# Loading and transposing the first sequence's z in three parts, and regrouping the first score tiles

## The chip, the core and the metric

The kernel runs on one core of a Trainium2 chip. The metric is the time of one execution on the device in microseconds: a median of 980.89 over three runs (980.73 to 981.65). The engines named below: TensorE (PE in the profile, its weight loads PEld), VectorE (DVE), ScalarE (ACT), GpSimd (POOL) and SyncE (SP). SP and POOL issue the DMAs, which all use the core's 16 DMA engines.

## What is computed

Eight sequences of 3072 rows each; z has 64 columns, u and v have 256. A squared-ReLU attention of z with itself, gated by u, is followed by a two-branch feed-forward layer.

```python
def _attn_ref(u, v, z):
    scores = (1.0 / S) * np.matmul(z, z.transpose(0, 2, 1))
    attn = np.maximum(scores, 0.0) ** 2
    return u * np.matmul(attn, v)

def _moe_ref(x, w1, w2, w_out):
    return np.maximum(x @ w1, x @ w2) @ w_out
```

The inputs are 32-bit floats in DRAM; the kernel computes in bf16 with 32-bit sums.

## The kernel before

**Tiles and steps.** A sequence is cut into 24 blocks of 128 rows. Four blocks of queries make a step, so there are six steps for a sequence and 48 in all. A step needs its scores against all 24 key blocks. Scores are made two key blocks at a time: a *pair* `k0` (key blocks k0 and k0+1) against the step's 512 queries, in one PSUM tile. The pair is passed through ReLU (ScalarE, or VectorE for a few pairs at the start, lines 215 to 218), then squared on VectorE (line 221) into `a_sb`. Then come four matmuls that add the pair's contribution to the two sums `xacc` (one for each half of v's 256 columns): I call them *adds*; they show as `xacc<-a_sb,v_sb`. Because the score matrix is symmetric, later steps reuse earlier pairs, turned by DMA transposes (`aT`).

**zT.** Scores need z transposed. `zT` has 25 slots of 128 x 128; slot s holds block s-1 in its lower 64 rows and block s in its upper 64. Scoring a pair with an even `k0` takes its weights from slot k0+1 and the first step's queries from slots 0 to 4. For later sequences zT is made by two DMA transposes (`make_zT`). For sequence 0 it is made by TensorE, with an identity matrix, in `zT_pe` (matmuls at line 134, the copy out of PSUM at line 135).

**The start, sequence 0.** SP loads the first nine blocks of z as 32-bit floats (line 336). POOL builds the identity, loads the other 15 blocks with a cast (line 342), then the six parts of v (four blocks each) and u for the first step. VectorE and ScalarE cast the nine blocks (lines 343 and 344). TensorE runs idle matmuls on a blank tile (`idle`), transposes slots 0 to 8, runs four more idle matmuls, scores pairs 0 and 2, transposes slots 9 to 24, and scores pairs 4 and 6; the order is written out by hand in lines 624 to 660.

**The order of the rest.** `work` is the list of work items in TensorE's order; an item of the first step is one key block, two adds. Score tiles are grouped into *windows* (lines 502 to 508): the first three windows have two pairs each, all later ones three. A planner gives each window a place in `work` ahead of which it is issued (`laid`). Windows 0 and 1 are issued by hand; window 2 (pairs 8 and 10) is `third()`, issued ahead of item 2. Windows 3 (pairs 12, 14, 16), 4 (18, 20, 22) and 5 stand ahead of items 6, 12 and 18. PSUM has three buffers (`mm_psum`) for score tiles and transposes; a buffer comes free when its ReLU or its copy has read it. TensorE takes its matmuls in program order.

**Transfers.** Loads and transposes of the later steps are planned by time (`plan`). A planned load on POOL first waits, in `gate`, for the tile that was made last (`fresh`), then is issued. SP's queue holds, in order, the first load of z, the transpose of u for the first step (`uT`), four `aT` transposes, and so on.

Of the kernel before, what the change touches and what calls it, by code (L numbers as in the profile page):

```python
# [11 lines left out]
def kernel(  # L12
# [17 lines left out]
    nc = tc.nc  # L30
    fp32 = mybir.dt.float32
    bf16 = mybir.dt.bfloat16
# [4 lines left out]
    dqk = z.shape[-1]  # L37
    Dff = moe_w1.shape[-1]

    P = 128  # L40
    NSB = S // P
    G = 4
    WIN = 3
# [12 lines left out]
    zepool = ctx.enter_context(tc.tile_pool(name="zepool", bufs=1))  # L56
# [11 lines left out]
    mm_psum = ctx.enter_context(tc.tile_pool(name="mm_psum", bufs=3, space=bass.MemoryType.PSUM))  # L68
    acc_psum = ctx.enter_context(tc.tile_pool(name="acc_psum", bufs=1, space=bass.MemoryType.PSUM))

    pin = tc.keep_in_program_order

    def matmul(*args, **kw):
        pin(nc.tensor.matmul(*args, **kw))  # L74

    def sp_dma(**kw):
        pin(nc.sync.dma_start(**kw))
# [7 lines left out]
    def load(**kw):  # L85
        pin(nc.gpsimd.dma_start(**kw))
# [16 lines left out]
    def new_v():  # L103
        return vpool.tile([P, NSB, D], bf16, name="v_sb")

    def load_v(b, v_sb, t0, n):
        load(
            out=v_sb[:, ds(t0, n), :],
            in_=v[b].rearrange("(p t) d -> p t d", p=P)[:, ds(t0, n), :],
        )  # L110

    def load_u(b, c):
        u_sb = ulpool.tile([P, G, D], bf16, name="u_sb")
        load(
            out=u_sb,
            in_=u[b].rearrange("(p t) d -> p t d", p=P)[:, ds(c * G, G), :],
        )
        return u_sb
# [10 lines left out]
    def zT_pe(zT, z_sb, s0, n, tpz=None):  # L129
        flat = z_sb.rearrange("p t d -> p (t d)")  # L130
        if tpz is None:
            tpz = mm_psum.tile([P, 8, P], bf16, name="tpz", tag="mm")
        for j in range(n):
            pin(nc.tensor.transpose(tpz[:, j, :], flat[:, ds((s0 + j) * dqk, P)], ident))  # L134
        return lambda copy: pin(copy(zT[:, ds(s0, n), :], tpz[:, :n, :]))
# [50 lines left out]
    def direct(b, i, j):  # L186
        return b == 0 and i < j <= NDIR


    def score(q, out_ps, j, k, s, q0, n):  # L190
        half = ds(j * dqk, dqk)
        matmul(
            out_ps,
            q.zT[half, k + 1 - j, :],
            q.zT[half, ds(G * s + 1 - j + q0, n), :],
            start=True,
            stop=True,
        )

    def turn(out_ap, in_ap):  # L200
        sp_dma(out=out_ap, in_=in_ap, transpose=True)


    def scores_pair(b, s, k0):
        q = seqs[b]
        s_ps = mm_psum.tile([P, 2, GW], fp32, name="s_ps", tag="mm")
        for j in range(2):
            score(q, s_ps[:, j, :], j, k0 + j, s, 0, G)
        yield
        a_sb = apool.tile([P, 2, GW], bf16, name="a_sb")  # L210
        r_sb = apool.tile([P, 2, GW], bf16, name="r_sb", bufs=3)

        head = b == 0 and s == 0 and k0 < 12
        keep = pin if head else lambda ins: None
        if head and k0 in (2, 10):
            keep(nc.vector.tensor_single_scalar(out=r_sb, in_=s_ps, scalar=0.0, op=ALU.max))
        else:
            keep(nc.scalar.activation(r_sb, s_ps, AF.Relu))  # L218
        if head:
            yield  # L220
        keep(nc.vector.tensor_mul(a_sb, r_sb, r_sb))  # L221
        gj = k0 // G
        if gj > s and not direct(b, s, gj):
            if (s, gj) not in q.T:
                q.T[s, gj] = tpool.tile([P, G, G, P], bf16, name="aT")
            turn(
                q.T[s, gj][:, ds(k0 - G * gj, 2), :, :].rearrange("p k q x -> p (k q) x"),
                a_sb.rearrange("p j q -> p (j q)"),
            )
        yield a_sb  # L230
# [96 lines left out]

    q = seqs[0]  # L330
    ZF = 9
    blank = consts.tile([P, GW], bf16)
    pin(nc.vector.memset(blank, 0.0))
    zf = opool.tile([P, G, D], fp32, name="o_sb").rearrange("p t (n d) -> p (t n) d", d=dqk)
    z_in = z[0].rearrange("(p t) d -> p t d", p=P)
    sp_dma(out=zf[:, :ZF, :], in_=z_in[:, :ZF, :])
    ident = consts.tile([P, P], bf16)
    make_identity(nc, ident)
    z_sb_0 = zepool.tile([P, NSB + 2, dqk], bf16, name="z_sb")
    pin(nc.gpsimd.memset(z_sb_0[:, 0:1, :], 0.0))  # L340
    pin(nc.gpsimd.memset(z_sb_0[:, NSB + 1 : NSB + 2, :], 0.0))
    load(out=z_sb_0[:, 1 + ZF : 1 + NSB, :], in_=z_in[:, ZF:, :])
    pin(nc.vector.tensor_copy(z_sb_0[:, 1:6, :], zf[:, :5, :]))  # L343
    pin(nc.scalar.copy(z_sb_0[:, 6 : 1 + ZF, :], zf[:, 5:ZF, :]))
    q.v = new_v()
    for t0 in range(0, NSB, G):
        load_v(0, q.v, t0, G)
    q.u_sb[0] = load_u(0, 0)
    q.zT = zpool.tile([P, NSB + 1, P], bf16, name="zT")


    fresh = [None]
# [149 lines left out]
    windows, room = [], 0  # L502
    for i, (n, k0) in enumerate(tiles):
        if not room or (k0 is None and room < 2):
            windows.append([])
            room = 2 if i < 6 else WIN
        windows[-1].append((n, k0))
        room = 0 if (n + 1) % NG == 0 and k0 == -1 else room - 1

    begins, t = [], 0  # L510
# [9 lines left out]
    def free(at):  # L520
        return all(end <= at - 860 or at + 1700 <= beg for beg, end in shared)
# [5 lines left out]
    def apart(at):  # L527
        n = max(n for n, beg in enumerate(starts) if beg <= at)
        return n >= LAG or (at - starts[n]) % (6 * 432) == 0

    spots = [
        i
        for i, at in enumerate(begins)
        if free(at) and apart(at) and work[i][1] is False and work[i][0]
    ]
    GAP_FIRST, GAP = 2100, 2500
    n_first = sum(n < NG for n, _ in tiles) // WIN
    laid = {}
    limit = t
    for w in reversed(range(len(windows))):  # L540
        limit = min([limit] + [due[r] for r in windows[w] if r in due])
        found = [i for i in spots if begins[i] <= limit]
        i = found[-1] if found else 0
# [58 lines left out]
    def scores_window(w):  # L602
        gens = []
        for n, k0 in windows[w]:
            st = steps[n]
            if k0 is None:
                gens.insert(0, (st, k0, scores_diag(st.b, st.s)))
            elif k0 >= 0:
                gens.append((st, k0, scores_pair(st.b, st.s, k0)))
        for st, k0, gen in gens:  # L610
            next(gen)
        for st, k0, gen in gens:
            st.scored[k0] = a = next(gen)
            fresh[0] = a[:, 0, 0:1] if k0 is not None else a[:, 0, 0, 0:1]
# [4 lines left out]
    def idle(n):  # L619
        for _ in range(n):  # L620
            matmul(steps[0].xacc[0], blank[:, :P], blank, start=True, stop=True)


    laid = {i: [w for w in ws if w > 2] for i, ws in laid.items()}
    idle(6)
    parts = [zT_pe(q.zT, z_sb_0, 0, 5), zT_pe(q.zT, z_sb_0, 5, ZF - 5)]
    for part, copy in zip(parts, (nc.vector.tensor_copy, nc.scalar.copy)):
        part(copy)
    idle(4)
    heads = {k0: scores_pair(0, 0, k0) for w in range(3) for _, k0 in windows[w]}  # L630

    def ahead(*k0s):
        for k0 in k0s:
            next(heads[k0])

    def squared(*k0s):
        for k0 in k0s:
            steps[0].scored[k0] = a = next(heads[k0])
            fresh[0] = a[:, 0, 0:1]

    ahead(0, 2)
    ahead(0, 2)
    tpz = mm_psum.tile([P, 2, 8, P], bf16, name="tpz", tag="mm")
    parts = [zT_pe(q.zT, z_sb_0, ZF + 8 * i, 8, tpz[:, i]) for i in range(2)]
    squared(0)
    for part, copy in zip(parts, (nc.scalar.copy, nc.vector.tensor_copy)):
        part(copy)
    ahead(4)
    idle(1)
    ahead(6)  # L650
    idle(2)
    ahead(4, 6)
    squared(2, 4)

    def third():
        ahead(8, 10)
        ahead(8, 10)
        squared(6, 8, 10)

    laid.setdefault(spots[0] + 2, []).insert(0, -1)  # L660
    for i, (_, _, fn, _) in enumerate(work):
        for w in laid.get(i, []):
            scores_window(w) if w >= 0 else third()
        while transfers and transfers[0][0] <= begins[i]:
            _, _, is_load, begin_transfer = transfers.pop(0)
            if is_load:
                gate(fresh[0])
            begin_transfer()
        fn()
# [30 lines left out]
```

## Time and profile before

| | us |
|---|---|
| median of 3 runs (lowest, highest) | 980.89 (980.73, 981.65) |
| the profiled execution | 981.47 |
| its span on the core | 979.70 |

| where in the span | us |
|---|---|
| first idle matmul | 1.19 |
| nine blocks of z landed (288 KB, issued 0.74) | 3.67 |
| first transpose on TensorE | 4.17 |
| first scores (pairs 0 and 2) | 6.53 |
| second set of transposes, 16 | 7.06 |
| first adds (pair 0) | 9.47 |
| window 2 (pairs 8 and 10) | 10.43 |
| window 3 (pairs 12, 14, 16) | 12.80 |
| first load of u landed (issued 5.26) | 15.5 |
| first DMA transpose (uT) issued, landed | 15.52, 21.8 |
| uT first read (xT on VectorE) | 22.71 |

The page is one profiled execution: part 1 gives the busy time of each engine, part 4 the chain of work that ended last, part 6 the DMA issues with their median time from issue to landing. The timeline lists instructions in order of time, merged where they follow each other: start, duration, engine, line, operation and tiles. The DMA view of a stretch lists the queues that moved packets in it (q0 is POOL's, q1 is SP's), each with packets, megabytes and the share of 16 engines, and the DMAs whose issue falls in it.

### The profile page before, as it was taken

The page shows a single profiled execution, that of the slowest core. Times are in us where ns is not written, and L with a number is a line of the kernel's source. Part 1 is how long each engine was busy: PE and PEld are TensorE (multiplying, and loading weights), DVE is VectorE, ACT ScalarE, POOL GpSimd, SP SyncE. Part 2 cuts the span into 40 slices and gives each one's busy share as a digit, 9 for nine tenths or more (in the row PEclk, how much of TensorE's full clock was granted, in tenths as well). Part 3 has the DMA queues.
Part 4 walks back from the last instruction along what each step waited for, and adds up shares of the span by engine and source line. Part 5 has one row for each costly group of instructions (what it writes and reads, how often), then busy time and mean ns, then how long its engine had stood idle before and what let it go on. Part 6 is the DMA issues. An engine that isn't in the chain of part 4 may idle for free.

```text
span 979.7 us, 14514 instructions
## 1 busy us (share of the span) xinstructions
PE 968.9 (99%) x5661; PEld 510.6 (52%) x5742; DVE 432.0 (44%) x681; ACT 442.4 (45%) x500; POOL 77.5 (8%) x228
## 2 busy tenths in 40 slices
PE   9999999999999999999999999999999999999998
PEld 3355545555455554555545564455545555445556
DVE  6654444443544435433445334444345443554322
ACT  6853454334643355433554335533355433654322
POOL 2011100110001100010000100011000110000000
PEclk9999999999999999999999999999999999999999
DMA  9988899986989979898788968789777896896521
GB/s 150 186 142 150 145 180 153 165 147 114 182 161 149 150 118 180 152 168 130 150 157 144 175 122 164 142 153 181 135 147 149 135 188 126 148 164 115 109 66 65
DMA packets 378517, 143.46 MB, mean 146 GB/s; under 512 B 356944, under 2 KB 358608, under 8 KB 378448
## 3 DMA queue, kind: packets, MB, share of 16 engines
q1 hardware_dynamic: 361888, 112.78, 61.3%
q0 software_dynamic: 16560, 29.74, 21.5%
q8 instruction: 45, 0.74, 0.3%
q14 instruction: 24, 0.20, 0.1%
HBM read 59.77 MB, written 25.17 MB: 87 GB/s over the span
## 4 chain that ended last, share of the span: by engine, by line
PE 99%; issue 1%; DMA 0%; DVE 0%
PE xacc L74 52%; PE o_ps L74 21%; PE d_ps L74 17%; PE s_ps L74 8%; DMA o_sb<-in_z_dram 0%; PE tpz L134 0%; PE w2o_ps L74 0%; DVE o_sb L317 0%; DVE z_sb L343 0%
## 5 line engine op out<-in xcount | busy, mean ns | idle before, releaser
L74 PEld LDWEIGHTS <-v_sb 128*128 128x128 bf16 x2304 | 216.0, 98 | 277.4 <-issue 40.5
L218 ACT ACTIVATE r_sb<-s_ps 128x1024 bf16<-128x1024 f32 x258 | 248.5, 1023 | 111.4 <-PE s_ps L74 111.4
L221 DVE TENSOR_TENSOR a_sb<-r_sb 128x1024 bf16<-128x1024 bf16 x260 | 179.3, 691 | 212.1 <-ACT r_sb L218 207.9
L74 PE MATMUL xacc<-a_sb,v_sb 128*128 128x512 bf16 x997 | 231.0, 379 | 2.3 <-issue 0.2
L74 PE MATMUL xacc<-aT,v_sb 128*128 128x512 bf16 x912 | 216.5, 379 | 0.0
L74 PE MATMUL o_ps<-w_out_sb,g_sb 128*128 128x256 bf16 x1536 | 199.1, 273 | 0.0
L74 PE MATMUL d_ps<-xT,w_sb 128*128 128x512 bf16 x751 | 172.7, 379 | 0.9
L74 PEld LDWEIGHTS <-g_sb 128*128 128x128 bf16 x1536 | 149.9, 98 | 27.6
L292 ACT ACTIVATE g_sb<-d_ps 128x1024 bf16<-128x1024 f32 x96 | 98.3, 1024 | 138.8 <-PE d_ps L74 138.8
L292 DVE TENSOR_SCALAR g_sb<-d_ps 128x1024 bf16<-128x1024 f32 x96 | 117.4, 1223 | 84.7 <-PE d_ps L74 81.3
L323 ACT COPY o_sb<-o_ps 128x512 f32<-128x512 f32 x94 | 55.1, 586 | 178.2 <-PE o_ps L74 178.2
L268 DVE SCALAR_TENSOR_TENSOR xT<-xacc,uT 128x512 bf16<-128x512 f32 x96 | 62.0, 683 | 137.4 <-PE xacc L74 137.4
L74 PEld LDWEIGHTS <-w_sb 128*128 128x128 bf16 x768 | 75.1, 98 | 88.7
L74 PE MATMUL s_ps<-zT 64*128 64x512 bf16 (+3 forms) x696 | 89.2, 359 | 0.1
L246 ACT ACTIVATE r_sb<-s_ps 128x896 bf16<-128x896 f32 x44 | 40.3, 917 | 97.9 <-PE s_ps L74 97.9
L74 PE MATMUL xacc<-aD,v_sb 128*128 128x512 bf16 x331 | 79.9, 379 | 2.6 <-issue 2.2
L74 PE MATMUL o_ps<-W2o_sb,xT 128*128 128x256 bf16 x384 | 73.3, 273 | 0.0
L248 DVE TENSOR_SCALAR r_sb<-s_ps 128x384 bf16<-128x384 f32 x44 | 24.5, 558 | 95.3 <-PE s_ps L74 95.3
L74 PEld LDWEIGHTS <-zT 64*128 64x128 bf16 x696 | 27.2, 94 | 62.2 <-issue 50.4
L83 POOL COPY gate_sb<-g_sb 128x1 bf16<-128x1 bf16 x44 | 8.3, 188 | 420.0 <-DVE g_sb L292 253.2
L74 PEld LDWEIGHTS <-xT 128*128 128x128 bf16 x384 | 37.6, 98 | 4.4
L83 POOL COPY gate_sb<-a_sb 128x1 bf16<-128x1 bf16 x48 | 9.7, 203 | 273.9 <-DVE a_sb L221 273.9
(37 smaller groups left out, 144.2 us busy)
## 6 DMA issues: line engine op xcount, KB each, us to landing
out_dram<-o_sb SPq DMA_DIRECT2D x47, 512.0 KB, 3.7
v_sb<-in_v_dram POOLq DMA_DIRECT2D x48, 256.0 KB, 5.7
u_sb<-in_u_dram POOLq DMA_DIRECT2D x48, 256.0 KB, 5.3
aT<-a_sb SPq DMA_TRANSPOSE x228, 3.7
z_sb<-in_z_dram POOLq DMA_DIRECT2D x7, 384.0 KB, 7.5
aD<-aD SPq DMA_TRANSPOSE x132, 2.4
w_sb<-in_moe_w_dram POOLq DMA_DIRECT2D x2, 512.0 KB, 6.5
uT<-u_sb SPq DMA_TRANSPOSE x48, 4.8
```

What stands on the lines that cost most here:

```text
L74: pin(nc.tensor.matmul(*args, **kw))
L83: pin(nc.gpsimd.tensor_copy(gate_sb, tile_ap))
L218: keep(nc.scalar.activation(r_sb, s_ps, AF.Relu))
L221: keep(nc.vector.tensor_mul(a_sb, r_sb, r_sb))
L246: nc.scalar.activation(r_sb, s_ps[:, 0:7, :], AF.Relu)
L248: nc.vector.tensor_single_scalar(out=r2_sb, in_=s2_ps[:, 2:5, :], scalar=0.0, op=ALU.max)
L268: nc.vector.scalar_tensor_tensor(out=xT[:, dc, :].rearrange("p (t q) -> p t q", q=P), in0=xacc[dc].rearrange("p (t q) -> p t q", q=P), sca ...
L292: nc.any.tensor_single_scalar(out=g_sb[:, nb : nb + 2, :], in_=d_ps, scalar=0.0, op=ALU.max)
L323: nc.any.tensor_copy(o_sb[:, ds(2 * th, 2), :], o_ps[:, :, :D])
```

## The change

Sequence 0's z comes in three parts now. SP loads five blocks as 32-bit floats. POOL loads the next eight as its first instruction, ahead of building the identity, and the last eleven behind the first part of v. The load of u moves ahead of v's last two parts. The two edge slots of z are cleared by VectorE instead of POOL.

TensorE transposes slots 0 to 4 ahead of the scores of pairs 0 and 2, and slots 5 to 12 behind them. Slots 13 to 24 are filled by two DMA transposes on SP, odd slots first; they stand in SP's queue ahead of uT. The first three windows are pairs 0 and 2, pair 4, and pairs 6, 8 and 10. The third is still issued ahead of item 2; windows 3 and 4 are placed by hand ahead of items 8 and 14; the later windows stay where they were. Idle matmuls go from 13 to 7, and pair 10's ReLU goes from VectorE to ScalarE.

```diff
-        if head and k0 in (2, 10):
+        if head and k0 == 2:
             keep(nc.vector.tensor_single_scalar(out=r_sb, in_=s_ps, scalar=0.0, op=ALU.max))
...
-    ZF = 9
+    ZF, ZP = 5, 13
...
+    def load_z_0(t0, n):
+        load(out=z_sb_0[:, ds(1 + t0, n), :], in_=z_in[:, ds(t0, n), :])
+
     sp_dma(out=zf[:, :ZF, :], in_=z_in[:, :ZF, :])
+    load_z_0(ZF, ZP - ZF)
     ident = consts.tile([P, P], bf16)
     make_identity(nc, ident)
...
-    load(out=z_sb_0[:, 1 + ZF : 1 + NSB, :], in_=z_in[:, ZF:, :])
-    pin(nc.vector.tensor_copy(z_sb_0[:, 1:6, :], zf[:, :5, :]))
-    pin(nc.scalar.copy(z_sb_0[:, 6 : 1 + ZF, :], zf[:, 5:ZF, :]))
+    pin(nc.vector.memset(blank, 0.0))
+    pin(nc.vector.memset(z_sb_0[:, 0:1, :], 0.0))
+    pin(nc.vector.memset(z_sb_0[:, NSB + 1 : NSB + 2, :], 0.0))
+    pin(nc.vector.tensor_copy(z_sb_0[:, 1:4, :], zf[:, :3, :]))
+    pin(nc.scalar.copy(z_sb_0[:, 4 : 1 + ZF, :], zf[:, 3:ZF, :]))
     q.v = new_v()
-    for t0 in range(0, NSB, G):
+    load_v(0, q.v, 0, G)
+    load_z_0(ZP, NSB - ZP)
+    for t0 in range(G, 4 * G, G):
         load_v(0, q.v, t0, G)
     q.u_sb[0] = load_u(0, 0)
+    for t0 in range(4 * G, NSB, G):
+        load_v(0, q.v, t0, G)
     q.zT = zpool.tile([P, NSB + 1, P], bf16, name="zT")
+    for s0 in (ZP, ZP + 1):
+        n = (NSB + 2 - s0) // 2
+        sp_dma(
+            out=q.zT[:, s0 : NSB + 1 : 2, :],
+            in_=z_sb_0.rearrange("p t d -> p (t d)")[:, ds(s0 * dqk, n * P)],
+            transpose=True,
+        )
...
-            room = 2 if i < 6 else WIN
+            room = {0: 2, 2: 1}.get(i, WIN)
...
-    laid = {i: [w for w in ws if w > 2] for i, ws in laid.items()}
-    idle(6)
-    parts = [zT_pe(q.zT, z_sb_0, 0, 5), zT_pe(q.zT, z_sb_0, 5, ZF - 5)]
-    for part, copy in zip(parts, (nc.vector.tensor_copy, nc.scalar.copy)):
-        part(copy)
-    idle(4)
+    laid = {i: [w for w in ws if w > 4] for i, ws in laid.items()}
+    for k, w in ((2, -1), (8, 3), (14, 4)):
+        laid.setdefault(spots[0] + k, []).insert(0, w)
...
+    idle(4)
+    zT_pe(q.zT, z_sb_0, 0, ZF)(nc.vector.tensor_copy)
+    idle(1)
     ahead(0, 2)
     ahead(0, 2)
-    tpz = mm_psum.tile([P, 2, 8, P], bf16, name="tpz", tag="mm")
-    parts = [zT_pe(q.zT, z_sb_0, ZF + 8 * i, 8, tpz[:, i]) for i in range(2)]
+    part = zT_pe(q.zT, z_sb_0, ZF, ZP - ZF)
+    idle(2)
     squared(0)
-    for part, copy in zip(parts, (nc.scalar.copy, nc.vector.tensor_copy)):
-        part(copy)
+    part(nc.scalar.copy)
     ahead(4)
-    idle(1)
-    ahead(6)
-    idle(2)
-    ahead(4, 6)
-    squared(2, 4)
+    ahead(4)
+    squared(2)
 
     def third():
-        ahead(8, 10)
-        ahead(8, 10)
-        squared(6, 8, 10)
-
-    laid.setdefault(spots[0] + 2, []).insert(0, -1)
+        ahead(6, 8, 10)
+        ahead(6, 8, 10)
+        squared(4, 6, 8, 10)
```

More of the change, by code (lines that the diff above doesn't have):

```diff
@@ L330 @@
     q = seqs[0]
-    ZF = 9
+    ZF, ZP = 5, 13
     blank = consts.tile([P, GW], bf16)
-    pin(nc.vector.memset(blank, 0.0))
     zf = opool.tile([P, G, D], fp32, name="o_sb").rearrange("p t (n d) -> p (t n) d", d=dqk)
+    z_sb_0 = zepool.tile([P, NSB + 2, dqk], bf16, name="z_sb")
     z_in = z[0].rearrange("(p t) d -> p t d", p=P)
+    def load_z_0(t0, n):
+        load(out=z_sb_0[:, ds(1 + t0, n), :], in_=z_in[:, ds(t0, n), :])
     sp_dma(out=zf[:, :ZF, :], in_=z_in[:, :ZF, :])
+    load_z_0(ZF, ZP - ZF)
     ident = consts.tile([P, P], bf16)
     make_identity(nc, ident)
-    z_sb_0 = zepool.tile([P, NSB + 2, dqk], bf16, name="z_sb")
-    pin(nc.gpsimd.memset(z_sb_0[:, 0:1, :], 0.0))
-    pin(nc.gpsimd.memset(z_sb_0[:, NSB + 1 : NSB + 2, :], 0.0))
-    load(out=z_sb_0[:, 1 + ZF : 1 + NSB, :], in_=z_in[:, ZF:, :])
-    pin(nc.vector.tensor_copy(z_sb_0[:, 1:6, :], zf[:, :5, :]))
-    pin(nc.scalar.copy(z_sb_0[:, 6 : 1 + ZF, :], zf[:, 5:ZF, :]))
+    pin(nc.vector.memset(blank, 0.0))
[3 more added lines that the diff above has]
+    pin(nc.scalar.copy(z_sb_0[:, 4 : 1 + ZF, :], zf[:, 3:ZF, :]))
     q.v = new_v()
-    for t0 in range(0, NSB, G):
+    load_v(0, q.v, 0, G)
+    load_z_0(ZP, NSB - ZP)
+    for t0 in range(G, 4 * G, G):
         load_v(0, q.v, t0, G)
     q.u_sb[0] = load_u(0, 0)
+    for t0 in range(4 * G, NSB, G):
+        load_v(0, q.v, t0, G)
     q.zT = zpool.tile([P, NSB + 1, P], bf16, name="zT")
+    for s0 in (ZP, ZP + 1):
[5 more added lines that the diff above has]
+        )
     fresh = [None]
```

## The prediction

> **What bounds the kernel now.** I read the page first: busy shares (part 1) and the chain that ended last (part 4).
>
> ```profile
> PE 968.9 (99%) x5661; PEld 510.6 (52%) x5742; DVE 432.0 (44%) x681; ACT 442.4 (45%) x500; POOL 77.5 (8%) x228
> ...
> PE 99%; issue 1%; DMA 0%; DVE 0%
> ```
>
> TensorE is busy all the way and the chain is TensorE's own. So no other engine sets the time after the start; what counts is when TensorE gets into its unbroken stream, and whether anything breaks that stream. The timeline shows where the stream begins (start, duration, what):
>
> ```profile
> 10.97 1.90 PE L74 MATMUL xacc<-a_sb,v_sb 128*128 128x512 bf16 x8
> ...
> 12.80 0.82 PE L74 MATMUL s_ps<-zT 64*128 64x512 bf16 x6
> ...
> 13.56 2.76 PE L74 MATMUL xacc<-a_sb,v_sb 128*128 128x512 bf16 x12
> ```
>
> The scores of key pairs 12, 14 and 16 (I call them window 3) start at 12.80, when 12 adds (xacc matmuls) are done. From there windows of 0.75 us and 12 adds (0.216 us each) follow without a gap, one every 3.45 us. The reader should keep 12.80 and the 12 adds: any shift of the end is the new start of window 3 minus 12.80, less 0.216 us for every add done by then beyond 12.
>
> The change moves the transposes for window 3 from TensorE to DMA, so the DMA views come next. Between 7 and 14 us:
>
> ```profile
> q0 software_dynamic: 793, 1.45, 111.2%
> ```
>
> That is all: POOL's loads fill the 16 DMA engines (packets overlap, hence over 100%) and nothing else moves. The v and u loads are issued by 5.86 us; the last, issued at 5.26, takes this long to land, that is until 15.5:
>
> ```profile
> u_sb<-in_u_dram POOLq DMA_DIRECT2D x1, 256.0 KB, 10.2
> ```
>
> What a DMA transpose does beside such loads is the question. Free of loads (73 to 77 us), two transposes of 13 and 12 tiles take
>
> ```profile
> zT<-z_sb SPq DMA_TRANSPOSE x2, 4.3
> ```
>
> Beside a load, 23 to 26 us, with a transpose of a_sb issued at 22.76:
>
> ```profile
> q0 software_dynamic: 212, 0.43, 97.4%
> issues: line engine op xcount, KB each, median us to landing
> aT<-a_sb SPq DMA_TRANSPOSE x1, 6.4
> ```
>
> Only q0 is listed: the transpose moved no packet in three microseconds, while the load (w2) drained. And with two loads queued ahead (164.4 to 166 us; z_sb issued at 164.27, aT at 164.46):
>
> ```profile
> z_sb<-in_z_dram POOLq DMA_DIRECT2D x1, 384.0 KB, 7.1
> aT<-a_sb SPq DMA_TRANSPOSE x1, 7.9
> ```
>
> The load lands at 171.4, the transpose at 172.35, 0.9 us behind it. The same pairing at 284 to 286, 404 to 406, 525 to 527, 645 to 647 and 765 to 767 us gives 0.75 to 1.0 us. The first transpose of the program (uT, issued 15.52) landed at 21.8, 2.5 us behind the u load issued just before it (19.3).
>
> **The change part by part.**
>
> *The head chain.* The first load falls from 9 to 5 blocks (288 to 160 KB), and landed at 3.67. Bounds for the new landing: 3.13 (its first engine now) to 3.9 (POOL's eight-block load is issued 0.75 us earlier and shares the engines); I take 3.4. Casts of 192 and 128 columns instead of 320 and 256 (0.33 and 0.41 us) give about 0.26 and 0.30. The first transpose came 0.48 us after the landing, now 0.41: 3.8. Five at 0.107 us; the copy of 640 columns started 0.72 us after the first transpose and takes 0.49: it ends at 5.05. The second copy (0.59, on ScalarE) and three of the four idle matmuls behind it go, so scores start at 5.1, not 6.53. Their matmuls still come at the early pitch of 0.43 us: relu 0 on ScalarE 5.75 to 6.8, the relu of pair 2 on VectorE (1.23) 6.2 to 7.4, square 0 until 8.1. Eight more transposes follow the scores (their blocks land near 5.5), and ScalarE copies them after relu 0: 7.05 to 8.06 (1.01).
>
> *What then limits is ScalarE.* Pair 4 is scored at 8.1, relu 4 runs 8.55 to 9.55, then pairs 6, 8 and 10 (pair 10's relu moves here from VectorE) at 0.95 us each: relu 10 ends at 12.65. TensorE meanwhile does 4 adds, the scores of 6, 8, 10 (three PSUM buffers; the third waits for relu 4), and 12 adds from 10.1 to 12.8. Window 3's last pair needs relu 10's buffer, 12.7. So TensorE reaches window 3 at **12.8, as before, but with 16 adds done**: -4 x 0.216 = **-0.86 us**. The 12 transposes and 6 idle matmuls that TensorE loses (18 fewer) all lie before this point, where the chain and not TensorE sets the time; they are worth nothing beyond it.
>
> *Window 5.* Windows 3 and 4 each move four adds later in the order, window 5 stays, so only 8 adds (1.73 us) lie between windows 4 and 5: 2.48 us, where ScalarE needs 2.85 for three relus. Window 5's third pair waits for a buffer: **+0.43 us**. The old order had 12 adds there and hides it.
>
> *The DMA transposes.* Eleven blocks are loaded behind v's first part: 352 KB read. POOL's queue starts 0.75 us earlier and reads 512 KB per 1.27 us (v landings: x6 with a median of 7.7 us from issue), so: eight blocks at about 5.4, v0 at 6.7 (first used 8.45), eleven blocks at about 7.5. Then SP may issue the first transpose, six tiles. At that time three v parts, u and two v parts are queued: 6 x 1.27 us more, last landing 15.3. The lower end for the transpose is 7.5 + 4.3 = 11.8 (no load beside it), the upper 15.3 + 2.5 = 17.8 (as uT), and a next load of u, issued near 14 when POOL's gate sees the square of pair 10, can go ahead of it too. Every transpose in the trace that met two loads landed behind them, by up to 1.0 us in the later stages and by 2.5 in this one; I take 1.3: **landing 16.6, window 3 at 16.65, not 12.80: +3.85 us**. Window 3's weights need exactly this transpose (slot 13 is its first); nothing behind them on TensorE can pass.
>
> *The rest of the queues.* SP: uT and the aT transposes now stand behind both zT transposes. If each issue holds SP for 4.34 us, as aT's did at 22.76, uT goes out near 16 and lands by 22.3; it is first read by xT, 22.71 before and 3.4 us later now. That hides it with 3.8 us to spare. The second zT transpose serves later query rows. v's last two parts land at 14.0 and 15.3 (12.96 and 14.3 before), needed from 17.9. POOL issues one more DMA (0.53) with nothing late behind it; ident is ready near 2.0. VectorE's two extra memsets lie in its wait for z.
>
> Sum: 3.85 - 0.86 + 0.43 = **+3.4 us**. The profiled execution took 981.47 (span 979.70), 0.58 over the median of 980.89; against the median: **984.3 us**.
>
> [...]
>
> **The rivals.**
> A, the forecast: the transpose waits for the loads; landing 15.3 to 17.8, 983.0 to 985.5.
>
> B, the same, and the stall costs more than itself. After the last matmul the windows view has
>
> ```profile
> 976.20:979.70 3.50, 0.09 (x1) 0.00 (x0) 0.42 (x1) 0.00 (x0) 0.00 (x0) 0.88 0.22 75
> ```
>
> The number behind the five engines' busy times is the granted clock: 0.88 is half rate for 0.84 of 3.5 us, so the clock fell some 2.6 us after TensorE stopped. A stall of 3.8 us is longer. Matmuls at half rate lose 0.21 us each; the only warm-up in the trace lasted from 1.19 to about 6.2, 5.0 us, a loss of up to 2.5; the lower end is nothing. I take 1.5, less 0.4 because ScalarE then keeps up in window 5: 985.4, and 988 with a late landing too, or with the next u load ahead of the transpose. Against it: only one fall is in the trace, and not every stall of that length need meet it. [...]
>
> C, not slower: the transposes do find turns between the loads. They land in time up to 12.75, and then only -0.86 + 0.43 is left: 980.5. Each microsecond of landing beyond adds one: the time of before is reached at 13.2, 0.2% (1.96 us) above it at 15.1. For it: in some stretches both queues move (18 to 18.5 us: 39 packets of q0, 119 of q1), and transposes free of loads are quick. Against it: the rows above.
>
> D, faster by over 0.2%: C, with ScalarE's chain 1.6 us shorter as well, 978.9. Five relus of 0.95 to 1.0 us and a copy of 1.01 between 5.75 and 12.65 leave no such room.
>
> That the change does something else is out: the two programs' instruction orders show these moves. Should the five blocks land no sooner, the wait for the transposes covers it.
>
> **How the numbers follow.** A 0.45, B 0.33, C 0.19, D 0.03. The forecast is A's 984.3. The range of 981.8 to 987.6 leaves out the lower part of C, D, and the tip of B. About 0.2% (979 to 982.8) is what a measurement of this kernel can tell from no change: slower is A and B, 0.78; same is C, 0.19; faster is D, 0.03.
>
> **What would show it.** The first score at 5.1; 16 adds before window 3; TensorE idle 3 to 5 us there with a DMA into zT as releaser; zT's landing some 9 us after issue while q0 alone moves packets until about 15; after it matmul pitch of 0.216 (A) or 0.43 (B). The forecast is wrong if zT's first landing lies before 13, or if window 3 waits for ScalarE instead.

## The result, and the profile after

The changed kernel took **987.73 us**, the median of 6 runs (986.76 to 994.33), against 980.94 for the kernel before (6 runs, 980.73 to 981.65): a ratio of 1.0075, 95% interval 1.0059 to 1.0092. It is slower, and 0.13 us beyond the upper end of the range on record. The profiled execution took 987.17, its span is 985.4, 5.7 us more than before.

Busy shares (part 1) and the chain that ended last (part 4) of the changed kernel's page:

```profile
PE 969.1 (98%) x5644; PEld 509.6 (52%) x5724; DVE 430.7 (44%) x681; ACT 442.5 (45%) x500; POOL 77.3 (8%) x227
...
PE 97%; DMA 1%; issue 1%; ACT 0%; POOL 0%; DVE 0%; POOLq 0%; ACTq 0%; SPq 0%
```

TensorE executes fewer instructions (5644, not 5661) and is busy as long as before (969.1 us, there 968.9). What is new is the 1% of DMA in the chain. The timeline of TensorE from window 2 on shows where it comes in (start, duration, line and tiles; in brackets the idle time before and what ended it):

```profile
9.88 2.76 PE L74 MATMUL xacc<-a_sb,v_sb 128*128 128x512 bf16 x12
17.58 1.46 PE L74 MATMUL s_ps<-zT 64*128 64x512 bf16 x6 [4.93 <-DMA zT<-z_sb]
...
22.57 0.82 PE L74 MATMUL s_ps<-zT 64*128 64x512 bf16 x6
23.32 1.90 PE L74 MATMUL xacc<-a_sb,v_sb 128*128 128x512 bf16 x8
25.16 1.14 PE L74 MATMUL s_ps<-zT 64*128 64x512 bf16 x6
26.23 2.76 PE L74 MATMUL xacc<-a_sb,v_sb 128*128 128x512 bf16 x12
28.93 0.82 PE L74 MATMUL s_ps<-zT 64*128 64x512 bf16 x6
```

The score lines are windows 3 (17.58), 4, 5 and 6. Three things are to be seen. TensorE stands still for 4.93 us ahead of window 3, and the releaser is a DMA into zT. Window 3 then takes 1.46 us instead of 0.82. And window 5 takes 1.14, with a gap in it. The windows view, cut where the granted clock changes (length, busy times of PE, PEld, DVE, ACT, POOL, then the clock), explains the second (TensorE's full clock shows as 1.00):

```profile
10.59:14.00 3.41, 2.06 (x10) 0.74 (x8) 2.08 (x3) 1.82 (x2) 0.72 (x2) 1.00 1.10 195
14.00:17.42 3.42, 0.00 (x0) 0.00 (x0) 0.00 (x0) 0.00 (x0) 0.00 (x0) 1.00 1.27 185
17.42:20.83 3.41, 3.04 (x10) 1.01 (x12) 1.32 (x2) 2.60 (x3) 0.00 (x0) 0.50 0.91 160
20.83:24.24 3.41, 3.41 (x20) 1.25 (x18) 0.94 (x3) 1.49 (x3) 0.00 (x0) 1.00 0.39 73
```

From 17.42 to 20.83 the clock is at half: just when zT has come and TensorE could go on.

Window 6 is a good ruler, because from there on the order of the work is that of before. In the timeline of before it is the line

```profile
23.15 0.82 PE L74 MATMUL s_ps<-zT 64*128 64x512 bf16 x6
```

It starts at 23.15 before and at 28.93 now, **5.78 us later**; the span is 5.7 longer. So all of the loss has been made by 29 us, and it adds up from terms that can be read off these lines: window 3 starts 17.58 - 12.80 = +4.78 later; it has 16 adds done ahead of it instead of 12, -0.86; window 4 comes 4.99 us after window 3 instead of 3.45, +1.54; window 5 is 0.32 longer. 4.78 - 0.86 + 1.54 + 0.32 = 5.78.

Why zT came so late: its first transpose was issued at 8.42 and landed at 17.53. From 8 to 12 us only POOL's queue moved packets (queue, packets, megabytes, share of 16 engines):

```profile
q0 software_dynamic: 398, 0.73, 108.6%
issues: line engine op xcount, KB each, median us to landing
zT<-z_sb SPq DMA_TRANSPOSE x2, 9.4
```

and from 12.5 to 15.5 both queues moved packets, 280 of POOL's and 347 of SP's:

```profile
q0 software_dynamic: 280, 0.51, 90.8%
q1 hardware_dynamic: 347, 0.09, 21.1%
```

The last of the loads queued ahead (v's last part) landed at 16.92, the transpose 0.61 us behind it.

### The profile page after: what moved, and what is told of

Read it like the earlier page. It is cut to its first block, busy times and chain, and to the rows that moved or that the text cites. A ratio compares the mean times of both kernels' runs of the same rounds, so it can differ in the third digit from the quotient of the medians.

```text
span 985.4 us, 14484 instructions
## 1 busy us (share of the span) xinstructions
PE 969.1 (98%) x5644; PEld 509.6 (52%) x5724; DVE 430.7 (44%) x681; ACT 442.5 (45%) x500; POOL 77.3 (8%) x227
## 4 chain that ended last, share of the span: by engine, by line
PE 97%; DMA 1%; issue 1%; ACT 0%; POOL 0%; DVE 0%; POOLq 0%; ACTq 0%; SPq 0%
PE xacc L74 51%; PE o_ps L74 21%; PE d_ps L74 17%; PE s_ps L74 8%; DMA zT<-z_sb 1%; DMA z_sb<-in_z_dram 1%; ACT r_sb L218 0%; PE w2o_ps L74 0%; POOL z_sb L86 0%; POOL v_sb L86 0%; DVE o_sb L317 0%; POOL ident masks.py:199 0%; POOL ident masks.py:197 0%; POOLq masks.py:199 0%; ACTq L218 0%
```

## The experiments

My theory: zT's DMA transpose ends behind the loads that were queued ahead of it, TensorE waits for it, and the wait costs about 1.5 us more than itself because the clock falls. Rivals: the transpose is slow by itself (some 9 us from its issue in any company); the new order or its regrouping costs the time; the transposes harm something else. All kernels below are the changed kernel with the edit shown, unless a line says that the edit stands on another one; times are medians beside the kernel before on the same chip. Every profiled one is held against the same ruler, window 6 at 23.15.

### No DMA transposes: TensorE makes slots 13 to 24

```diff
-    for s0 in (ZP, ZP + 1):
-        n = (NSB + 2 - s0) // 2
-        sp_dma(
-            out=q.zT[:, s0 : NSB + 1 : 2, :],
...
-            transpose=True,
-        )
...
+        if i == spots[0] + 5:
+            tpz = mm_psum.tile([P, 2, 6, P], bf16, name="tpz", tag="mm")
+            for h in range(2):
+                for j in range(6):
+                    src = z_sb_0.rearrange("p t d -> p (t d)")[:, ds((ZP + 6 * h + j) * dqk, P)]
+                    pin(nc.tensor.transpose(tpz[:, h, j, :], src, ident))
+            rest = q.zT[:, ds(ZP, 12), :].rearrange("p (h j) q -> p h j q", h=2)
+            pin(nc.vector.tensor_copy(rest, tpz))
```

> The changed kernel with slots 13 to 24 transposed by TensorE too (12 transposes behind six adds of window 2, copied by VectorE), no DMA transpose of z in the first sequence. If the DMA transposes are the whole loss: no stall, no fall of the clock; -0.86 and -0.15 for the earlier start, +0.43 at window 5, +0.7 for 12 transposes: 981.1. If the regrouped windows and the shorter first load cost by themselves: several microseconds above 981.

982.11 (10 runs, 981.53 to 982.29), ratio 1.0007 (0.9998 to 1.0017). Its timeline:

```profile
11.93 1.24 PE L74 MATMUL xacc<-a_sb,v_sb 128*128 128x512 bf16 x5
13.92 0.82 PE L74 MATMUL s_ps<-zT 64*128 64x512 bf16 x6 [0.75 <-DVE zT L674]
```

Window 6 starts at 23.73, +0.58. So 5.2 of the 5.78 us belong to the DMA transposes. The rest of the change (the first load, the order, the regrouping) costs little: window 3 at 13.92 is +1.12, of which 0.75 is a wait for VectorE's copy that my edit brought in; 1.12 - 0.86 + 0.32 = 0.58. That the order itself is the loss has fallen.

### Fewer loads ahead of the transposes

The loads of u and of v's last two parts are issued in `third()`, behind POOL's gate on the square of pair 10.

```diff
-    q.u_sb[0] = load_u(0, 0)
-    for t0 in range(4 * G, NSB, G):
-        load_v(0, q.v, t0, G)
...
         squared(4, 6, 8, 10)
+        gate(fresh[0])
+        load_v(0, q.v, 4 * G, G)
+        q.u_sb[0] = load_u(0, 0)
+        load_v(0, q.v, 5 * G, G)
```

> The changed kernel with three of the loads that stood in POOL's queue ahead of the transposes' turn (the first u and v's last two parts) issued behind a gate on the square of pair 10, near 13.4 us. If DMA transposes wait for the loads that are queued: the last load in the way is v's fourth part (12.6), zT lands at 13.5 to 14, the stall is 1 to 1.5 us, the clock stays up, 981 to 982. If the transpose is slow by itself (9 us from issue, whatever is queued): it lands at 17.5 and the time stays near 987.

983.04 (10 runs, 981.47 to 990.14), ratio 1.0027 (1.0007 to 1.0047). The transpose is issued at the same time as in the changed kernel (8.45, there 8.42), but lands at 13.34, not 17.53: 0.83 us behind v's fourth part, now the last load ahead of it (12.51). Between 12.5 and 13.5 us its queue is alone:

```profile
q1 hardware_dynamic: 814, 0.20, 104.3%
```

The timeline:

```profile
13.38 0.82 PE L74 MATMUL s_ps<-zT 64*128 64x512 bf16 x6 [0.86 <-DMA zT<-z_sb]
...
23.19 0.82 PE L74 MATMUL s_ps<-zT 64*128 64x512 bf16 x6
24.97 1.02 PE L74 MATMUL xacc<-a_sb,v_sb 128*128 128x512 bf16 x3 [0.95 <-DVE xT L268]
```

Window 6 is back at 23.19, **+0.04: the whole loss is gone** with the loads that stood ahead, and the clock does not fall (1.00 from 12.4 to 20 us). The rival of a transpose slow by itself has fallen: same issue, same size, 4.9 us instead of 9.1. But the time is not back: u was held too long, and the wait moves to uT. VectorE's timeline says so:

```profile
24.22 0.69 DVE L268 SCALAR_TENSOR_TENSOR xT<-xacc,uT 128x512 bf16<-128x512 f32 x1 [1.54 <-DMA uT<-u_sb]
```

### The held loads in another order, u first and earlier

u goes ahead of v's last two parts, behind the gate on the square of pair 8; the next load of u is planned 7 us later, so that it doesn't meet uT; window 4 stands ahead of item 13 instead of 14. As in the experiment before, the three loads are taken out further up; the lines below leave that out. The edit also moves `plan_load` out of the `if`, so the last step loads its u once more (49 loads of u, not 48, the last issued at 940.06); nothing waits for that load.

```diff
-        squared(4, 6, 8, 10)
+        squared(4, 6, 8)
+        gate(fresh[0])
+        q.u_sb[0] = load_u(0, 0)
+        load_v(0, q.v, 4 * G, G)
+        load_v(0, q.v, 5 * G, G)
+        squared(10)
...
-            plan_load(b, s, 2 if b == 0 else 4, lambda nx=nx: fetch_u(nx.b, nx.s))
+            at_u = (9 if s == 0 else 2) if b == 0 else 4
+        plan_load(b, s, at_u, lambda nx=nx: fetch_u(nx.b, nx.s))
...
-    for k, w in ((2, -1), (8, 3), (14, 4)):
+    for k, w in ((2, -1), (8, 3), (13, 4)):
```

> The changed kernel with the first u and v's last two parts issued behind the square of pair 8 (12.2 us), u first; the second u load planned at 9 instead of 2 us, out of uT's way; window 4 one key block earlier (ahead of item 13). If zT waits for the loads queued ahead: v's fourth part lands at 12.5, zT at 13.3, window 3 at 13.4 with 16 adds done; uT in time for xT, no late buffer in window 5: 0.6 - 0.86 = -0.3 us, 980.9 beside 981.2 of before. If the loads held back only move the collision: a stall for uT or for v's fifth part, 982 or more.

981.67 (12 runs; ten from 981.33 to 983.64, two at 987.43 and 989.71), ratio 1.0019 (1.0003 to 1.0034). In its profile

```profile
13.69 0.82 PE L74 MATMUL s_ps<-zT 64*128 64x512 bf16 x6 [1.51 <-DMA zT<-z_sb]
...
19.73 0.82 PE L74 MATMUL s_ps<-zT 64*128 64x512 bf16 x6
...
23.18 0.82 PE L74 MATMUL s_ps<-zT 64*128 64x512 bf16 x6
```

Window 3 has lost 0.89 and won 0.86. Window 5 (19.73) takes 0.82 again now that ten adds lie between windows 4 and 5 instead of eight, so the late buffer was a matter of these adds. Window 6 is at +0.03 and the profiled span 0.1 shorter than before. The change's gains and costs cancel even when the transposes come in time.

### Still fewer loads ahead, and the transposes earlier

First, v's fourth part is held as well, behind the gate on the square of pair 4 (on top of the kernel just before):

```diff
-    for t0 in range(G, 4 * G, G):
+    for t0 in range(G, 3 * G, G):
         load_v(0, q.v, t0, G)
...
-        squared(4, 6, 8)
+        squared(4)
+        gate(fresh[0])
+        load_v(0, q.v, 3 * G, G)
+        squared(6, 8)
```

> As the kernel with u held back, with v's fourth part held back too, behind the square of pair 4 (10.0 us). The last load ahead of zT is then v's third part (11.0): zT at 11.8 to 12.6, window 3 at 12.65 without a wait and with 16 adds done: -0.15 - 0.86 = -1.0 us, 980.2 beside 981.2 of before. If the fourth part's packets, from 11.4 on, go ahead of the transpose: it lands behind 14.7, at 15.5, and the time is 983 to 985. If transposes take 5 us from issue in any case: 13.3 and 981.

984.29 (12 runs, 981.88 to 991.3), ratio 1.0037 (1.002 to 1.0054). Window 3 starts at 12.73, near the forecast of 12.65, after a wait of 0.39 us for zT. But the held part now meets the second transpose of zT, and TensorE waits 0.75 us for v, 2.8 us later on for xT and uT, and 2.1 us far from the change for a transpose of the diagonal (aD):

```profile
18.90 1.04 PE L74 MATMUL xacc<-a_sb,v_sb 128*128 128x512 bf16 x4 [0.75 <-DMA v_sb<-in_v_dram]
...
40.73 4.18 PE L74 MATMUL xacc<-a_sb,v_sb 128*128 128x512 bf16 x12 [2.79 <-DVE xT L268]
...
218.45 1.50 PE L74 MATMUL xacc<-aD,v_sb 128*128 128x512 bf16 x6 [2.14 <-DMA aD<-aD]
```

Window 6 is at +0.17, and the two later waits, with a fall of the clock at the first of them (12 adds in 4.18 us, not 2.76), come on top. This profiled execution took 988.14, 3.9 us more than the median, so not every execution can have had all of them. Holding loads moves the collision.

Second, in the changed kernel again, the loads stay, but the last eleven blocks of z go ahead of v's first part, so that the transposes can be issued sooner:

```diff
-    load_v(0, q.v, 0, G)
     load_z_0(ZP, NSB - ZP)
+    load_v(0, q.v, 0, G)
```

> The changed kernel with the load of the last eleven blocks ahead of v's first part, so that SP issues the transpose some 1.3 us earlier. If it waits for the loads queued behind it anyway: zT still lands behind v's last part, 16.8 to 17.5, time 986.5 to 988. If its time from issue is what counts (9.1 us): it lands at 16.2, the stall is 1.3 us shorter, 985.5 or 984 if the clock then stays up.

998.73 and 986.55 (2 runs; the first is the profiled one). The issue comes 2.2 us sooner (6.26) and the landing 0.85 us *later*: 18.38, 12.1 us from issue, 0.26 behind v's last part (18.12).

```profile
18.43 0.82 PE L74 MATMUL s_ps<-zT 64*128 64x512 bf16 x6 [3.00 <-DMA zT<-z_sb]
```

Window 6 is at +6.77. With the same loads queued an earlier issue bought nothing. In five profiles, the landings (us) of zT's first transpose and of the last load queued ahead:

| kernel | issued | last load | zT | behind it |
|---|---|---|---|---|
| changed | 8.42 | 16.92 | 17.53 | 0.61 |
| z ahead of v's first part | 6.26 | 18.12 | 18.38 | 0.26 |
| u and v's last parts held | 8.45 | 12.51 | 13.34 | 0.83 |
| the same, u first | 9.03 | 12.80 | 13.65 | 0.85 |
| v's fourth part held too | 8.72 | 11.17 | 12.69 | 1.52 |

From issue to landing it is 4.0 to 12.1 us; behind the last load it is 0.3 to 1.5. In three further profiles with all loads ahead (idle matmuls, the repeat and the unused transposes, all below) it is 0.58 to 0.65. The 1.52 need not be a wait for the loads: 3.97 us from issue is no longer than the 4.3 of the transposes without loads, so there the transpose's own time can decide. The kernel before shows the same order throughout: 56 of its DMA transposes were issued with two of POOL's loads more than 0.5 us from landing, and each landed behind the later one, by 0.24 to 5.1 us.

### What the clock's fall costs

TensorE is kept busy while it waits: 22 idle matmuls ahead of window 3 read a blank tile, and nobody reads what they write.

```diff
+            if w == 3:
+                warm = mm_psum.tile([P, GW], fp32, name="warm", tag="mm")
+                for _ in range(22):
+                    matmul(warm, blank[:, :P], blank, start=True, stop=True)
```

> The changed kernel with 22 idle matmuls on a spare PSUM tile ahead of window 3, to fill the stall. If the stall itself lets the clock fall: no fall in this run, zT lands at 17.5 as before, window 3 starts near 17.6 and takes 0.8 us instead of 1.4, window 4 follows 3.45 us later instead of 5.0; the end moves by about -1.5 us against the changed kernel, to 986. If the clock falls for another reason, or if its fall costs nothing, the time stays at 987.7.

988.04 (4 runs: 985.57, 986.71, 989.37, 991.14), ratio 1.0068 (1.0044 to 1.0092): the times scatter too far to show 1.5 us. The mean granted clock of each execution sorts them: 1.000 in those of 985.57 and 986.71, 0.998 in those of 989.37 and 991.14, so the idle matmuls did not keep the clock up everywhere in these two. The profiled execution (985.57) shows the price:

```profile
12.35 4.91 PE L74 MATMUL warm<-blank 128*128 128x512 bf16 x21
17.52 0.82 PE L74 MATMUL s_ps<-zT 64*128 64x512 bf16 x6 [0.25 <-DMA zT<-z_sb]
...
27.32 0.82 PE L74 MATMUL s_ps<-zT 64*128 64x512 bf16 x6
```

Window 3 starts when it did in the changed kernel (17.52, there 17.58), but takes 0.82 us, and window 6 is at +4.17 instead of +5.78: 4.72 - 0.86 + 0.32 = 4.18, with no term for the clock. So the fall is worth 1.6 us (5.78 - 4.17), and the wait less the four adds 3.9 (4.72 - 0.86).

The changed kernel once more, to see how steady the fall is:

> The changed kernel itself, on the chip of the two kernels beside it, to see how far its times spread: 987 to 988 in most executions if the stall for zT and the fall of the clock are all there is; some at 990 and above if the shift of the start upsets later transfers too, as one execution (994.3) let suspect.

988.75 (4 runs, 988.12 to 989.65), ratio 1.0078 (1.0065 to 1.0091). Window 3 starts at 17.35, a little sooner, yet window 6 is at +6.74: the clock is at half for 6.83 us, twice as long. The windows view, cut on this run's clock:

```profile
12.77:16.18 3.41, 0.54 (x3) 0.04 (x1) 0.81 (x2) 0.31 (x1) 0.72 (x2) 1.00 1.19 199
16.18:19.59 3.41, 2.02 (x8) 0.59 (x10) 0.54 (x1) 1.59 (x2) 0.00 (x0) 0.50 1.27 174
19.59:23.01 3.42, 3.42 (x9) 1.22 (x9) 1.54 (x3) 1.26 (x2) 0.00 (x0) 0.50 0.33 55
```

4.55 - 0.86 + 0.32 = 4.01; the remaining 2.73 is the clock. The two lengths show in the mean granted clock of the other executions too: over both rounds, the three at 0.998 took 986.76 to 987.24, the six at 0.996 or 0.997 took 988.12 to 989.65, and the one of 994.33 has 0.993.

### The transposes without the wait

As in the first experiment TensorE makes the slots, but the two DMA transposes are issued as well, into a buffer that nobody reads.

```diff
+    idle_T = zpool.tile([P, NSB + 1, P], bf16, name="zT")
+    for s0 in (ZP, ZP + 1):
+        sp_dma(
+            out=idle_T[:, s0 : NSB + 1 : 2, :],
+            in_=z_sb_0.rearrange("p t d -> p (t d)")[:, ds(s0 * dqk, 6 * P)],
+            transpose=True,
+        )
```

> The kernel of e3_pe (TensorE makes slots 13 to 24), and beside it the change's two DMA transposes, with the same reads and at the same place of SP's queue, into a buffer that nobody reads. Their transfers and their place ahead of uT are those of the changed kernel; only the wait of TensorE is gone. If the cost of the changed kernel is TensorE's wait for zT, this takes what e3_pe took: window 3 at 13.9, the window after window 5 0.6 us later than before, median near 982.1, whenever the transposes land (near 17.4). If the transposes disturb something else as well (SP's queue, the loads behind them, uT), it takes more by that: uT late by about 1 us gives 983, and the single executions 6 to 12 us longer, which the kernels with an early transpose of z showed in 1 of 6 executions and e3_pe in none of 10, come back. If those belong to TensorE's wait or to the clock's fall at it, they stay away.

982.06 (11 runs, 981.7 to 984.96), ratio 1.0013 (1.0004 to 1.0022). The transposes landed at 17.87 and 21.43, as late as ever, and it cost next to nothing:

```profile
14.06 0.82 PE L74 MATMUL s_ps<-zT 64*128 64x512 bf16 x6 [0.75 <-DVE zT L681]
...
23.87 0.82 PE L74 MATMUL s_ps<-zT 64*128 64x512 bf16 x6
```

Window 6 is at +0.72, from a window 3 that came 0.14 later than in the first experiment. uT lands at 23.77, and VectorE waits 0.5 us for it, TensorE 0.16. So **what costs the time at the start is TensorE's wait, not the transfers**. Three of the eleven executions took 984.0 to 985.0, which the first experiment never did, and none took more.

### TensorE's transposes with the copy cut in two

```diff
-            pin(nc.vector.tensor_copy(rest, tpz))
+            pin(nc.vector.tensor_copy(q.zT[:, ds(ZP, 6), :], tpz[:, 0]))
+            squared(10)
+            pin(nc.scalar.copy(q.zT[:, ds(ZP + 6, 6), :], tpz[:, 1]))
```

(On top of the first experiment; `third()` stops at the square of pair 8, and window 4 stands ahead of item 13.)

> e3_pe with the copy of the twelve TensorE transposes cut in two: slots 13 to 18 by VectorE ahead of the square of pair 10, slots 19 to 24 by ScalarE behind the ReLU of pair 10; window 4 stands ahead of item 13, not 14. If e3_pe's remaining 0.6 us is the wait of window 3 for VectorE's copy (0.75 us) and the late buffer of window 5 (0.3), both go: window 3 at about 13.2 with 16 adds done, and the window after window 5 about 0.5 us earlier than before (22.7), span 979.2, median 980.7 to 981.1. If window 3 then waits for a buffer or for the copy's start instead, it stays near 13.9 and the median near 981.8.

981.00 (11 runs, 980.53 to 981.9), where before took 981.5 on the same chip (21 runs): ratio 0.9998 (0.9989 to 1.0007). In the profile

```profile
12.73 0.82 PE L74 MATMUL s_ps<-zT 64*128 64x512 bf16 x6
...
22.22 0.82 PE L74 MATMUL s_ps<-zT 64*128 64x512 bf16 x6
```

Window 3 comes at 12.73 with 16 adds done and without a wait, window 6 at 22.22: **-0.93**, as -0.07 - 0.86 says, and the span is 978.8, 0.9 shorter than before. It is the fastest profile of this study, but the difference is within what the times can tell.

## Why the prediction was wrong

The direction, the place and the mechanism were right: TensorE waits ahead of window 3 for zT's first DMA transpose, which lands behind the loads queued ahead of it. The step that failed is the term for the clock: the sum put it at nothing. The forecast was taken from rival A, "the transpose waits for the loads", and B, "the same, and the stall costs more than itself", was given 0.33 only. The clock fell at this stall in all three profiles in which TensorE waited behind the full set of loads (the changed kernel, its repeat, z first), and did not where idle matmuls kept TensorE busy; it cost 1.54 us in the profile that the sum is held against. A second term, the landing, was short by 0.9.

Point by point, against the sum 3.85 - 0.86 + 0.43 = 3.4:

| term | forecast | measured |
|---|---|---|
| z's first load landed, first scores | 3.4, 5.1 | 3.08, 4.73 |
| TensorE could start window 3, with | 12.8, 16 adds | about 12.65, 16 adds |
| last load ahead landed | 15.3 | 16.92 |
| zT behind it | 1.3 | 0.61 |
| window 3 later by | 3.85 | 4.78 |
| four adds done ahead of it | -0.86 | -0.86 |
| window 5's late buffer | 0.43 | 0.32 |
| clock | 0 (B: 1.5) | 1.54 |
| sum | 3.4 | 5.78 |

*The clock* is the larger miss, 1.54 of 2.36 us. The prediction had the row for it (a fall 2.6 us after the last matmul) and its price, 1.5, and said that a stall of 3.8 us is longer; it still went against its own row, because "not every stall of that length need meet it". The waits that met one and those that did not are listed below, and the stall came out longer than 3.8 us. The 3.41 us at half clock cost 1.54, the repeat's 6.83 us 2.73; TensorE was still waiting in the first 0.16 us of the one and the first 1.17 us of the other.

*The landing* is 0.9 late out of two misses that partly cancel. The last load came 1.6 later than estimated: z's last eleven blocks landed at 8.34, not 7.5, and the six loads behind them took (16.92 - 8.34) / 6 = 1.43 us each, not 1.27. (The prediction's own terms, 7.5 and 6 x 1.27, give 15.1 and not 15.3.) In the last experiment, without DMA transposes of z, the six took (16.30 - 8.51) / 6 = 1.30. So the loads took 0.13 us longer each in the profile with the transposes beside them. The transpose's packets, which the trace shows from 12.39 us on, can be a part of it only: one load landed 1.76 us behind the one before it (9.57 to 11.33) when the transpose had been issued but had moved no packet, and what slowed it is open. What the prediction read of the later stages, a landing up to 1.0 us behind two loads, holds for the pairings that it names; a transpose of z that the kernel before issued at 188.66 landed at 197.23, 5.0 us behind the second of two loads (192.23).

*Window 5* lost 0.32, not 0.43; the prediction's own two figures, 2.85 and 2.48, give 0.37. It lost the same 0.32 where the clock did not fall (idle matmuls, u and v held), so B's relief of 0.4 by the fall is not there.

*ScalarE* did not set the time ahead of window 3: pair 10's ReLU ended at 12.41, TensorE's sixteenth add at 12.64. Both lie near the forecast's 12.8, so the term came out right.

*Nothing else is late*, as forecast: uT landed at 20.51 and was read at 28; v's parts were in time.

C (the transposes land in time: 980.5, reaching the time of before at a landing of 13.2) did not happen, but was built with the loads held and u first: window 3 at 13.69 without the late buffer gave +0.03.

*Against the median* the forecast took the profiled execution as 0.58 over it, as before; here the profiled one is 0.56 under. So 1.14 of the 3.43 us between 984.3 and 987.73 have nothing to do with the mechanism: they come of which execution was profiled. The changed kernel's executions scatter (986.76 to 994.33, where the fall's length alone makes 1.2 us between the two profiles), and the range reached to 987.6.

**What stays open.** Single executions of kernels in which a transpose of z stands early in SP's queue took 6 to 12 us more than their fellows: 994.33 in 1 of 6 of the changed kernel, 2 of 10 and 2 of 12 with held loads, 998.73 of the order with z first. With v's fourth part held, 4 of 12 took 987.75 to 991.3, beside 981.88 for the shortest, and with idle matmuls 2 of 4 took 4 to 6 us more than the shortest. The kernel before (69 executions) and the two without these transposes (21) never did. All these long executions have a mean granted clock of 0.993 to 0.998, lower than their fellows but for one (988.14 has 0.998, as one of 984.27 has), as further stalls of TensorE would give. In two that have a profile the stall can be seen: TensorE waits near 218 us, far from the change, for a transpose of the diagonal (aD), for 8.6 us in the execution of 998.73, where the loads beside it are slow, and for 2.1 us in that of 988.14. With transposes that nobody waits for, none of 11 did, but three took 2 to 3 us more. That is too few to say whether the wait or the transfers bring the large ones, and what links the change to a stall 200 us later was not shown.

## What to carry to other kernels

A DMA transpose that was put behind queued loads was worth its landing here, not its issue: it landed 0.26 to 1.52 us behind the last load queued ahead, in five profiles with issues from 6.26 to 9.03. So ask which load queued ahead lands last, and put the consumer there. When such a wait leaves TensorE idle for as long as those that met the clock's fall here, add the fall to its price (1.54 and 2.73 us in two profiles) instead of treating it as a side case: all five profiled waits of 2.79 us or more met it, and none of 2.14 us or less did. And before work is moved off a busy engine, see whether the engine was what set the time at that place: the matmuls that the change took from TensorE ahead of window 3 were worth nothing, and 12 transposes back on TensorE, with their copy split, gave the shortest span.

## What was not expected of the hardware

**When the clock falls, and for how long.** The changes of the clock that were read off these profiles lie whole multiples of 3.41 us apart within a run, at other places in each run: in the changed kernel it falls at 17.42 and is back at 20.83; in the repeat it falls at 16.18, is back at 23.01 and falls, behind the last matmul, at 985.57, 284 steps of 3.4133 us behind the first fall; with z first it falls at 19.30 and at 224.10, 60 steps apart. 17.42 is no whole step from 16.18. The counts that follow are of stretches of 3.41 us cut at these places. A stretch at full clock in which TensorE was busy for 0.00, 0.54, 0.87 or 1.09 us (the changed kernel, its repeat, z first, v's fourth part held) was followed by one at half clock; 2.04, 2.06, 2.64 or 2.96 us were followed by full clock. The two closest cases are the end of the kernel with u first, where 1.38 us were followed by half clock, and the long wait with z first, where 1.42 us were followed by full:

```profile
974.93:978.34 3.41, 1.38 (x13) 0.99 (x11) 0.42 (x1) 0.37 (x1) 0.00 (x0) 1.00 0.43 143
978.34:979.58 1.24, 0.00 (x0) 0.00 (x0) 0.00 (x0) 0.00 (x0) 0.00 (x0) 0.50 0.00 0
...
217.27:220.69 3.42, 1.42 (x7) 0.55 (x6) 0.00 (x0) 0.00 (x0) 0.00 (x0) 1.00 1.18 116
220.69:224.10 3.41, 0.00 (x0) 0.00 (x0) 0.00 (x0) 0.00 (x0) 0.00 (x0) 1.00 2.09 77
```

So the fall came without a wholly idle stretch too. An estimate from these figures (the busiest stretch before a fall, 1.38 us, and the idlest read here without one, 1.42): a stretch with less than about 1.4 us of work, that is with more than 2.0 us of idle time, brings the fall; by it a wait under 2.0 us would not meet it by itself, one over 4.0 us would, and between them it would depend on where the wait lies. The profiled waits fit it, but no run was made to test it. A stretch at half clock with 2.94, 3.04 or 3.19 us of work was followed by full; the repeat's, with 2.02, by another at half. So the changed kernel's stall of 4.93 us cost 1.54 us of clock and the repeat's of 4.04 us 2.73; that the place of the stall makes the difference is an estimate from these stretches. The wait of 2.79 us with v's fourth part held met the fall:

```profile
36.85:40.26 3.41, 1.09 (x8) 0.31 (x7) 0.27 (x1) 2.05 (x3) 0.00 (x0) 1.00 1.17 216
40.26:43.67 3.41, 2.94 (x7) 0.99 (x7) 3.41 (x6) 1.02 (x1) 0.00 (x0) 0.50 1.06 201
```

**A transpose beside queued loads.** In the changed kernel it moved no packet in the 3.9 us from its issue at 8.42 to 12.3 us, while POOL's queue moved 392. From 12.02 to 15.5 us SP's queue moved 349 packets and POOL's 335, and from 15.5 to 17.6, when POOL's had 45 left, SP's moved 1204. Issued 2.2 us sooner (z first) the transpose landed 0.85 us later. With fewer loads queued its packets came sooner: with u and v's last two parts held, the first within 2.1 us of the issue (31 of them from 10 to 10.5 us, and 1600 by 13.5 us, where the changed kernel had moved 121 by 14), and with v's fourth part held too within 1.4 us (25 from 9.9 to 10.1). How the engines choose between the two queues was not shown.
